# Reordering the head of a fused attention and gated-FFN kernel: new landing assumptions, short holds, a random tie-break, and a last output tile cut 384 and 128 wide

## The chip, the cores and the metric

One core of one Trainium2 chip. The metric is the device time of one execution in microseconds (us). All executions used here are in the fast state. A profile's span, from first to last instruction, is about 1.8 us shorter than the device time of the same execution; spans are compared with spans, times with times.

## The reference

Block-sparse attention with 4 batches, 8 heads, 768 positions and head size 64 feeds a gated FFN. In short:

```python
scores = scale * np.matmul(q, k.transpose(0, 1, 3, 2))
# mask: neighbouring 32-blocks, first and last block, three sampled blocks a row
scores = np.where(mask, scores, -1000000000.0)
attn = np.exp(scores - scores.max(-1, keepdims=True))
attn = attn / (attn.sum(-1, keepdims=True) + 1e-09)
x = np.matmul(attn, v)                      # to 3072 tokens x 512
gate = 1.0 / (1.0 + np.exp(-(x @ w_gate)))
return (gate * (x @ w_val) @ w_out)         # d_ff is 1536
```

## The kernel before

The kernel doesn't write its instructions in the order in which they run. It records operations, each with an engine, an assumed duration and a priority, and its own planner plays them through and gives each engine its order. What the planner assumes of the loads therefore decides where the TensorE's instructions stand; the chip then keeps that order, whatever really lands when. Cut to what matters:

```python
# Plan.run: on each engine, the first ready operation by (priority, place in the program)
for i, o in enumerate(self.ops):
    o.key = (o.prio, i)
...
# if the TensorE has nothing ready, it gets a filler: a matmul on a tile of zeros
if best is None and e == "PE" and now < self.spin_until and ...:
    o = self.spin_op(0.11 if now < 12.0 else 0.06, fresh)
...
# when a load is assumed to have landed
first = now + (2.5 if e == "POOL" else 1.9)
...
o.seen = first + 0.3 + o.slack

# the order of the first loads on one queue (head pairs 0 to 3)
FIRST = [
    ("q", 0), ("k", 1), ("q", 1), ("k", 2), ("q", 2), ("v", 0), ("k", 3), ("q", 3), ("v", 1), ("v", 2), ("v", 3),
]

# the last output tile, two pieces of 256 columns
parts = 2 if last and tt == w // 128 - 1 else 1
wd = DM // parts
for u in range(parts):
    m = slice(u * wd, u * wd + wd)
```

Below, k3 is the k of head pair 3, and so on. A score tile is one third of the keys of one head pair and query group; a value group is the 24 matmuls that follow three exponentials; gate matmuls are those with wg and wv.

The softmax here doesn't subtract the row's maximum and nothing guards it: scores larger than these inputs give would overflow.

Of the kernel before, what the change touches and what calls it, by code (L numbers as in the profile page):

```python
# [22 lines left out]
DM = H * D  # L23
# [4 lines left out]
VW = 66  # L28
SPIN = 22.0
NMASK = 1  # L30
Q0P, M1P, M2P = -39.2, 14, 17
XR, HR = 4, 2
EARLY = [(0, 0), (1, 0), (0, 1), (0, 2), (0, 3)]
FETCH = ((6, 1), (1, 2))
CHAIN, GLAG, OLAG, ROUND = 16, 5, 9, "SoVgggoo"
EDGES = [0, 768, 1536]
LAND = dict(sbi=1.7, mi=1.6, ident=3.2, e0=3.4, e1=3.3, q=3.1, kb=4.4, k=3.5)
FIRST = [
    ("q", 0), ("k", 1), ("q", 1), ("k", 2), ("q", 2), ("v", 0), ("k", 3), ("q", 3), ("v", 1), ("v", 2), ("v", 3),
]  # L40
HALF = [(0, 0), (0, 1), (0, 2), (0, 3)]
TURN_PE = 3
# [19 lines left out]
class Op:  # L62
    def __init__(self, ways, deps, allocs, prio, mode, dma, behind, lands):
        self.ways, self.deps, self.allocs = ways, deps, allocs
        self.prio, self.mode, self.dma, self.behind, self.lands = prio, mode, dma, list(behind), lands
        self.eng = self.start = self.end = self.seen = None
        self.paired = False
        self.slack = 0.0


LAT = {"PE": 0.35, "ACT": 0.2, "DVE": 0.2, "POOL": 0.25, "SP": 0.1}
# [2 lines left out]
class Plan:  # L74
# [35 lines left out]

    def run(self):
        todo = {e: [] for e in LAT}
        for i, o in enumerate(self.ops):
            o.key = (o.prio, i)
            for e in o.ways:
                todo[e].append(o)
        for e in todo:
# [4 lines left out]
        dma_free, mode, order, now = 0.0, None, [], 0.0  # L122
# [48 lines left out]
        while left:  # L171
            wake = []
            for e in LAT:
                if free[e] > now:
                    wake.append(free[e])
                    continue
                best = None
                for o in todo[e]:
                    t = 0.0
                    for d in o.deps:  # L180
                        if d.seen is None:
                            t = None
                            break
                        t = max(t, d.seen if d.eng != e or d.dma else d.end)
                    if t is None or any(d.end is None for d in o.behind):
                        continue
                    if t > now:
                        wake.append(t)
                        continue
                    t, where = places(o.allocs, e)  # L190
                    if t is None:
                        continue
                    if t > now:
                        wake.append(t)
                        continue
                    if o.mode == "row" and mode == "full" and o.paired:
                        s, _ = places([o.allocs[0], o.twin], e)
                        if s is None or s > now:
                            if s is not None:
                                wake.append(s)  # L200
                            if best is None:
                                best = o, where
                            continue
                    best = o, where
                    break
                if best is None and e == "PE" and now < self.spin_until and self.spin.writers[0].seen is not None:
                    if self.spin.writers[0].seen <= now:
                        fresh = self.spun is None or self.rings["ps"][self.spun.slot] is not self.spun
                        o = self.spin_op(0.11 if now < 12.0 else 0.06, fresh)
                        t, where = places(o.allocs, e)  # L210
                        if t is not None and t <= now:
                            best = o, where
                            todo[e].append(o)
                            left += 1
                        elif fresh:
                            self.spun = None
                if best is None:
                    continue
                o, where = best
                take(o, where)  # L220
                o.eng = e
                dur, o.fn = o.ways[e]
                if e == "PE":
                    if o.mode != mode:
                        dur += 0.095
                    mode = o.mode
                o.start, o.end = now, now + dur
                if o.lands is not None:
                    o.seen = o.lands
                    dma_free = max(dma_free, o.lands - 0.3) if e == "POOL" else dma_free  # L230
                elif o.dma:
                    first = now + (2.5 if e == "POOL" else 1.9)
                    if o.dma > 0.15:
                        first = dma_free = max(dma_free, first) + o.dma
                    o.seen = first + 0.3 + o.slack
                else:
                    o.seen = o.end + LAT[e]
                free[e] = o.end
                for w in o.ways:
                    todo[w].remove(o)  # L240
                order.append(o)
                left -= 1
                wake.append(o.end)
            ahead = [w for w in wake if w > now]
            if not ahead:
                if left and not wake:
                    raise RuntimeError("the plan is stuck")
                if left and all(w <= now for w in wake):
                    raise RuntimeError("the plan is stuck")
                continue  # L250
            now = min(ahead)
# [13 lines left out]
def kernel(  # L265
# [11 lines left out]
    nc = tc.nc  # L277
# [21 lines left out]
    P = Plan()  # L299
# [39 lines left out]
    ident16 = one([128, 128], f16, "ident16")  # L339
# [15 lines left out]
    for i, (eng, q, r) in enumerate((("SP", nc.sync, 0), ("ACT", nc.scalar, 64))):  # L355
# [3 lines left out]
            writes=[e24], prio=-93, dma=0.2, lands=LAND[f"e{i}"],  # L359
        ).deps[1:] = []  # L360
    vring = [one([128, 2, NJ, VW], f16, f"v16_{i}") for i in range(8)]
    for i in range(8):
# [3 lines left out]
            writes=[vring[i]], prio=-80 + i,  # L366
# [57 lines left out]
    def load_half(nm, b, p, prio, dur=0.72):  # L424
        cut = (nm, b, p) == ("q", 0, 0)
        js = later if cut else every
        if cut:
            c = one([128, 2, NJ - 2, 64], f16, "q16_late")
        else:
            c = sb(f"{nm}16" if nm != "v" else "vh", [128, 2, NJ, 64], f16)  # L430
        half16[nm, b, p] = stage[nm, b, p] = c
        o = P.op(
            "POOL", dur, lambda: nc.gpsimd.dma_start(c(), src[nm][b][:, 2 * p : 2 * p + 2, js]),  # L433
            writes=[c], prio=prio, dma=0.8 if cut else 1.0,
        )
        o.slack = 0.4 + 0.6 * b
        return o

    def turn_pe(nm, b, p, js, prio, behind=(), c=None, j0=0):
# [47 lines left out]
    P.op("ACT", 0.35, lambda: nc.scalar.copy(q_a(), q_in()), reads=[q_in], writes=[q_a], prio=-88)  # L487
    for i, (nm, p) in enumerate(FIRST):
        last_in = load_half(nm, 0, p, -60 + i)
    late = None  # L490
    for p in range(NP):
        if p == 0:
# [16 lines left out]
    n = 0  # L509
    for a, z in zip(edges, edges[1:]):  # L510
        for nm, t, s in (("g", wg, wgv), ("v", wv, wvv)):

            def go(t=t, s=s, a=a, z=z, nm=nm):
                landed[nm, a] = nc.gpsimd.dma_start(t()[:, :, a:z], s[:, :, a:z])

            o = P.op("POOL", 0.75, go, prio=-37.5 + n * 0.75, behind=[last_in], dma=32 * (0.022 + (z - a) * 0.000124))
            n += 1
            for f in range(a // 128, z // 128):
                w_in[nm, f] = o

    def load_out(s, prio, behind):
        def go():
            ins = nc.gpsimd.dma_start(wo()[:, 4 * s : 4 * s + 4], wov[:, 4 * s : 4 * s + 4])
            if s == 1:
                landed["o"] = ins

        o = P.op(
            "POOL", 0.8, go,
            prio=prio, dma=2.65, behind=behind,
        )  # L530
        for f in range(4 * s, 4 * s + 4):
            w_out[f] = o

# [83 lines left out]
    def attend(n, p, seq):  # L617
        b, c = divmod(n, NCH)
        masked = n < NMASK
        pts = []  # L620
        for tt in range(NCH):
            st, pt = psb([2, 512], homes=PAIR, span=2), sb("pt", [128, 2, 2, CH], f16)

            def scores(tt=tt, st=st):
# [16 lines left out]
                writes=[st], prio=seq, mode="row", behind=scored[-1:],  # L641
            )
            if (n, p, tt) == (0, 0, 0):
# [8 lines left out]
                reads=[st], writes=[pt], prio=seq,  # L652
# [14 lines left out]
        def values():  # L667
# [9 lines left out]
                        )  # L677

        valued[n, p] = P.op("PE", 0.79, values, reads=[*pts, v16[b, p]], writes=[o], prio=seq + (3.05 if n == 0 and p < 3 else 0.1), mode="full")
        P.op("DVE", 0.2, lambda: nc.vector.reciprocal(rz(), o()[:, :, 64:65]), reads=[o], writes=[rz], prio=seq - 5)  # L680
        P.op(
            "DVE", 0.36,
            lambda: nc.vector.tensor_tensor(  # L683
# [3 lines left out]
                op=ALU.mult,  # L687
            ),
            reads=[o, rz], writes=[x16], prio=seq - 5,
        )  # L690
        g, i = group_of[n]
        dst = xT[g, p]
        if n >= TURN_PE:
# [11 lines left out]
        def turn():  # L705
# [1 line left out]
            for jq in range(2):  # L707
                nc.tensor.transpose(tT()[:, jq, :], x16()[:, jq, :], ident16())  # L708

        P.op("PE", 0.12, turn, reads=[x16, ident16], writes=[tT, dst], prio=seq - 5, mode="full")  # L710
        P.op(
            "DVE", 0.28,
            lambda: nc.vector.tensor_copy(  # L713
                dst()[:, i * CH : (i + 1) * CH], tT().rearrange("p j q -> p (j q)")
            ),
            reads=[tT], writes=[dst], prio=seq - 5,
        )


    hts, gates, outs = {}, [], []  # L720
# [1 line left out]
    def ffn(g, seq):  # L722
# [42 lines left out]
        for tt in range(w // 128):  # L765
            n, jq = GROUPS[g][tt // 2], tt % 2
            b, c = divmod(n, NCH)
            y = sb("y", [128, DM], f32)
            parts = 2 if last and tt == w // 128 - 1 else 1
            wd = DM // parts  # L770
            for u in range(parts):
                m = slice(u * wd, u * wd + wd)
                py = psb([DM])
                for f0 in range(0, NF, 2):

# [112 lines left out]
```

## Time and profile before

| what | value |
|---|---|
| time, median of 3 | 292.07 us (291.51 to 292.13) |
| span of the profile | 290.4 us |
| TensorE busy | 284.0 us, 98% |
| first score matmul, first gate matmul | 6.47 us, 28.74 us |
| first output matmul of the third group | 90.53 us |
| start of the last matmul to the end | 3.38 us |

The starts are read off the TensorE's timeline. The prediction shows the lines of the page, the waits and the chain.

### The profile page before, as it was taken

The page shows a single profiled execution, that of the slowest core. Times are in us where ns is not written, and L with a number is a line of the kernel's source. Part 1 is how long each engine was busy: PE and PEld are TensorE (multiplying, and loading weights), DVE is VectorE, ACT ScalarE, POOL GpSimd, SP SyncE. Part 2 cuts the span into 40 slices and gives each one's busy share as a digit, 9 for nine tenths or more (in the row PEclk, how much of TensorE's full clock was granted, in tenths as well). Part 3 has the DMA queues.
Part 4 walks back from the last instruction along what each step waited for, and adds up shares of the span by engine and source line. Part 5 has one row for each costly group of instructions (what it writes and reads, how often), then busy time and mean ns, then how long its engine had stood idle before and what let it go on. Part 6 is the DMA issues. An engine that isn't in the chain of part 4 may idle for free.

```text
span 290.4 us, 8113 instructions
## 1 busy us (share of the span) xinstructions
PE 284.0 (98%) x3410; PEld 211.8 (73%) x3410; DVE 192.5 (66%) x448; ACT 211.1 (73%) x330; POOL 14.9 (5%) x24
## 2 busy tenths in 40 slices
PE   7899999999999999999999999999999999999995
PEld 6576876787687677777777767767777777777763
DVE  3778979778775767657857867756765765763230
ACT  2958689988957778678779779678768777772331
POOL 8740000000000000000000000000000000000000
PEclk9999999999999999999999999999999999999999
DMA  7999999996686484015286686011011010111003
GB/s 112 176 208 210 208 250 225 274 257 208 142 198 208 61 232 84 19 47 205 50 236 144 167 238 102 18 47 45 18 50 42 14 56 23 36 56 45 9 30 109
DMA packets 50788, 35.30 MB, mean 122 GB/s; under 512 B 31376, under 2 KB 47808, under 8 KB 50752
## 3 DMA queue, kind: packets, MB, share of 16 engines
q1 hardware_dynamic: 43304, 27.71, 37.1%
q0 software_dynamic: 7232, 7.01, 15.0%
q8 instruction: 26, 0.43, 0.6%
q14 instruction: 10, 0.08, 0.1%
q10 hardware_dynamic: 216, 0.07, 0.1%
HBM read 28.42 MB, written 6.29 MB: 120 GB/s over the span
## 4 chain that ended last, share of the span: by engine, by line
PE 93%; DMA 3%; POOL 2%; DVE 1%; issue 0%; ACT 0%; POOLq 0%
PE psum L734 44%; PE psum L778 23%; PE psum L672 13%; PE psum L631 12%; DMA k<-in_k_dram 3%; PE psum L708 1%; PE psum L451 1%; POOL k L433 0%; POOL q L433 0%; PE psum L593 0%; POOL k_a L480 0%; POOL q_late L433 0%; POOL k_b L484 0%; POOL vh L433 0%; DVE mask L601 0%
## 5 line engine op out<-in xcount | busy, mean ns | idle before, releaser
L649 ACT ACTIVATE pt<-psum 128x1024 f16<-128x1024 f32 x144 | 138.2, 1031 | 20.6 <-PE psum L631 20.5
L657 DVE TENSOR_TENSOR pt<-pt,mask 128x1024 f16<-128x1024 f16 x132 | 89.0, 688 | 50.1 <-ACT pt L649 50.0
L734 PE MATMUL psum<-x,wv 128*128 128x256 f16 x576 | 86.4, 273 | 0.0
L734 PE MATMUL psum<-x,wg 128*128 128x256 f16 x576 | 86.3, 272 | 0.0
L753 ACT ACTIVATE tg<-psum 128x256 f32<-128x256 f32 x144 | 56.4, 393 | 39.3 <-PE psum L734 39.2
L760 DVE SCALAR_TENSOR_TENSOR h<-tg,psum 128x256 f16<-128x256 f32 x144 | 58.2, 417 | 26.0 <-ACT tg L753 25.5
L778 PE MATMUL psum<-wo,h 128*128 128x512 f16 (+1 forms) x300 | 75.1, 372 | 0.0
L734 PEld LDWEIGHTS <-wv 128*128 128x128 f16 x576 | 56.0, 98 | 7.0 <-issue 0.6
L734 PEld LDWEIGHTS <-wg 128*128 128x128 f16 x576 | 53.5, 98 | 7.3 <-issue 0.6
L672 PEld LDWEIGHTS <-pt 128*128 128x128 f16 x1152 | 42.4, 98 | 9.4 <-issue 0.8
L631 PE MATMUL psum<-qT,kT 64*128 64x256 f16 x576 | 44.3, 271 | 0.3 <-DVE x L713 0.3
L672 PE MATMUL psum<-v,pt 128*128 128x65 f16 x1152 | 44.5, 193 | 0.0
L778 PEld LDWEIGHTS <-h 128*128 128x128 f16 x300 | 26.2, 98 | 23.1 <-issue 7.4
L631 PEld LDWEIGHTS <-kT 64*128 64x128 f16 x576 | 24.5, 94 | 19.5 <-issue 15.9
L795 ACT ACTIVATE y<-psum 128x512 f32<-128x512 f32 (+1 forms) x24 | 13.9, 579 | 13.0 <-PE psum L778 13.0
L683 DVE TENSOR_TENSOR x<-psum,rz 128x256 f16<-128x256 f32 x48 | 20.3, 424 | 1.5
L680 DVE RECIPROCAL rz<-psum 128x4 f32<-128x4 f32 x48 | 8.6, 179 | 3.5 <-PE psum L672 3.4
L374 PE MATMUL psum<-zero 128*64 128x128 f16 x40 | 5.4, 300 | 1.0 <-DVE zero L344 1.0
L601 DVE TENSOR_SCALAR mask<-psum 128x512 f16<-128x512 f32 x9 | 6.2, 686 | 0.3 <-PE psum L593 0.2
L631 PE MATMUL psum<-bias,e 64*128 64x256 f16 x48 | 6.1, 275 | 0.0
L421 ACT CAST q<-qs 128x768 f16<-128x768 f32 x7 | 5.9, 849 | 0.0
L374 PEld LDWEIGHTS <-zero 128*64 128x64 f16 x40 | 4.3, 163 | 1.7 <-DVE zero L344 1.0
(54 smaller groups left out, 72.1 us busy)
## 6 DMA issues: line engine op xcount, KB each, us to landing
out_dram<-y SPq DMA_DIRECT2D x23, 256.0 KB, 2.4
ks<-in_k_dram SPq DMA_DIRECT2D x12, 384.0 KB, 3.6
qs<-in_q_dram SPq DMA_DIRECT2D x12, 384.0 KB, 4.3
vs<-in_v_dram SPq DMA_DIRECT2D x12, 384.0 KB, 5.7
wg<-in_moe_w_gate_dram POOLq DMA_DIRECT2D x2, 768.0 KB, 14.3
wv<-in_moe_w_val_dram POOLq DMA_DIRECT2D x2, 768.0 KB, 16.4
wo<-in_moe_w_out_dram POOLq DMA_DIRECT2D x3, 512.0 KB, 22.3
vh<-in_v_dram POOLq DMA_DIRECT2D x4, 192.0 KB, 7.8
```

The source lines that it names most:

```text
L374: "PE", dur, lambda: nc.tensor.matmul(t()[0:64], zero()[:, 0:64], zero(), start=True, stop=True),
L631: nc.tensor.matmul(st()[:, hd, jj * CH : (jj + 1) * CH], l[r, 2 * tt + jj, :], m[r, 2 * c : 2 * c + 2, :], start=not (own and masked), sto ...
L649: lambda st=st, pt=pt: nc.scalar.activation(pt().rearrange("p h j q -> p h (j q)"), st(), AF.Exp, scale=SCALE),
L657: nc.vector.tensor_tensor(t, t, mask()[:, c, tt].unsqueeze(1).to_broadcast([128, 2, 512]), op=ALU.mult)
L672: nc.tensor.matmul(o()[:, 2 * jq + hd, 0:65], pts[j // 2]()[:, hd, j % 2, jq * 128 : jq * 128 + 128], v_[:, hd, j, 0:65], start=(j == 0), ...
L680: P.op("DVE", 0.2, lambda: nc.vector.reciprocal(rz(), o()[:, :, 64:65]), reads=[o], writes=[rz], prio=seq - 5)
L683: lambda: nc.vector.tensor_tensor(x16().rearrange("p j (h d) -> p (j h) d", d=64), o()[:, :, 0:64], rz().to_broadcast([128, 4, 64]), op=AL ...
L734: nc.tensor.matmul(t()[:, z : z + w], wt()[:, i, f * 128 : (f + 1) * 128], xT[g, i]()[:, 0:w], start=(i == 0), stop=(i == NP - 1),)
L753: lambda tg=tg, a=pair[0]: nc.scalar.activation(tg()[:, 0:w], a[0]()[:, a[1] : a[1] + w], AF.Tanh, scale=0.5),
L760: lambda tg=tg, a=pair[1], h_=h_: nc.vector.scalar_tensor_tensor(h_()[:, 0:w], tg()[:, 0:w], 1.0, a[0]()[:, a[1] : a[1] + w], op0=ALU.add, ...
L778: nc.tensor.matmul(py()[:, m], hts[g, f]()[:, tt * 128 : (tt + 1) * 128], wo()[:, f, m], start=(f == 0), stop=(f == NF - 1),)
L795: lambda py=py, y=y, m=m: nc.scalar.activation(y()[:, m], py()[:, m], AF.Copy, scale=0.5),
```

## The change

The intent is to plan with landing times closer to what was measured, so that the TensorE meets no load that has not landed: more slack for the loads of the first batch and of the weights (a little less, 0.7 instead of 1.0, for the second batch's), v1 fetched before k3 and q3, and engines that wait up to 0.4 us for the operations that follow a value group of the first query group, rather than let others overtake them. A fixed random draw breaks ties between priorities. The last output tile is cut so that less is left after the last matmul. The core of the diff, with cuts marked by "...":

```diff
+SEED, MIX = 17, 0.4
-XR, HR = 4, 2
+XR, HR, HOLD, HN = 4, 2, 0.4, 1
...
-    ("q", 0), ... ("q", 2), ("v", 0), ("k", 3), ("q", 3), ("v", 1), ("v", 2), ("v", 3),
+    ("q", 0), ... ("q", 2), ("v", 0), ("v", 1), ("k", 3), ("q", 3), ("v", 2), ("v", 3),
...
+        mix = np.random.default_rng(SEED).normal(0.0, MIX, len(self.ops))
         for i, o in enumerate(self.ops):
-            o.key = (o.prio, i)
+            o.key = (o.prio + (mix[i] if -45 < o.prio < 60 else 0.0), i)
...
+                        if t <= now + o.hold:
+                            break
...
-        o.slack = 0.4 + 0.6 * b
+        o.slack = 0.7
...
+        last_in.slack = 0.7 if i < 6 else 1.7
...
+            o.slack = 2.0          # the loads of wg, wv and wo
...
+        hold = HOLD if n < HN else 0.0   # on the four operations after a value group
...
-            parts = 2 if last and tt == w // 128 - 1 else 1
-            wd = DM // parts
-            for u in range(parts):
-                m = slice(u * wd, u * wd + wd)
+            cuts = [0, 384, DM] if last and tt == w // 128 - 1 else [0, DM]
+            for a, z in zip(cuts, cuts[1:]):
+                m, parts = slice(a, z), DM / (z - a)
```

More of the change, by code (lines that the diff above doesn't have):

```diff
@@ L38 @@
 FIRST = [
-    ("q", 0), ("k", 1), ("q", 1), ("k", 2), ("q", 2), ("v", 0), ("k", 3), ("q", 3), ("v", 1), ("v", 2), ("v", 3),
+    ("q", 0), ("k", 1), ("q", 1), ("k", 2), ("q", 2), ("v", 0), ("v", 1), ("k", 3), ("q", 3), ("v", 2), ("v", 3),
 ]
@@ L67, in __init__ @@
         self.paired = False
-        self.slack = 0.0
+        self.slack = self.hold = 0.0
 LAT = {"PE": 0.35, "ACT": 0.2, "DVE": 0.2, "POOL": 0.25, "SP": 0.1}
@@ L530, in load_out @@
         )
+        o.slack = 2.0
         for f in range(4 * s, 4 * s + 4):
@@ L679, in attend @@
         valued[n, p] = P.op("PE", 0.79, values, reads=[*pts, v16[b, p]], writes=[o], prio=seq + (3.05 if n == 0 and p < 3 else 0.1), mode="full")
-        P.op("DVE", 0.2, lambda: nc.vector.reciprocal(rz(), o()[:, :, 64:65]), reads=[o], writes=[rz], prio=seq - 5)
+        hold = HOLD if n < HN else 0.0
+        P.op(
+            "DVE", 0.2, lambda: nc.vector.reciprocal(rz(), o()[:, :, 64:65]), reads=[o], writes=[rz], prio=seq - 5
+        ).hold = hold
         P.op(
@@ L689, in attend @@
             reads=[o, rz], writes=[x16], prio=seq - 5,
-        )
+        ).hold = hold
         g, i = group_of[n]
@@ L708, in turn @@
                 nc.tensor.transpose(tT()[:, jq, :], x16()[:, jq, :], ident16())
-        P.op("PE", 0.12, turn, reads=[x16, ident16], writes=[tT, dst], prio=seq - 5, mode="full")
+        P.op("PE", 0.12, turn, reads=[x16, ident16], writes=[tT, dst], prio=seq - 5, mode="full").hold = hold
         P.op(
@@ L716, in attend @@
             reads=[tT], writes=[dst], prio=seq - 5,
-        )
+        ).hold = hold
     hts, gates, outs = {}, [], []
```

## The prediction

> **What bounds the kernel now.** I began with the page's busy shares and slices, to see whether one engine is full and where it is not.
>
> ```profile
> span 290.4 us, 8113 instructions
> ...
> PE 284.0 (98%) x3410; PEld 211.8 (73%) x3410; DVE 192.5 (66%) x448; ACT 211.1 (73%) x330; POOL 14.9 (5%) x24
> ...
> PE   7899999999999999999999999999999999999995
> ...
> PEclk9999999999999999999999999999999999999999
> ```
>
> The TensorE is busy in nearly all of every slice from the fourth to the last but one, at full clock. Only the first three slices (22 us) and the last show any slack. Busy is not the same as useful, so I next asked for the waits of the TensorE, in the whole run and from 40 us on. The second answer is empty; the first is this:
>
> ```profile
> PE psum L451 <- DMA k<-in_k_dram: 1.1, 1, 1.1
> PE psum L374 <- DVE zero L344: 1.0, 1, 1.0
> PE psum L569 <- DMA e<-bb_e: 0.6, 1, 0.6
> PE psum L593 <- ACT pt L649: 0.3, 1, 0.3
> PE psum L631 <- DVE x L713: 0.3, 1, 0.3
> ```
>
> The waits for the zero tile and for e are the start, which the change leaves as it is. What is left is 1.1 us for the k of the fourth head pair (k3) and twice 0.3 us. The chain of work in order of time shows where they stand and what the end is made of:
>
> ```profile
> 7.01 7.69 DMA k<-in_k_dram
> 14.70 0.04 issue
> 14.75 0.53 PE psum L451 x12
> 15.27 0.87 PE psum L672 x24
> ...
> 27.27 0.60 DVE mask L601
> 27.88 0.21 DVE x L713
> 28.08 0.04 issue
> 28.13 0.68 PE psum L631 x8
> 28.81 0.98 PE psum L734 x8
> ...
> 281.20 6.09 PE psum L778 x40
> ```
>
> The first gate matmuls (L734) start at 28.7 us, and from there the chain is TensorE alone down to the last output tile; after it come one 0.38 us eviction (287.31 to 287.69) and the last store, issued at 287.72 and landed at 289.42. So the kernel is a fixed amount of TensorE work, a head of 28.7 us with some holes, and a tail of 3.1 us. The change can win only the holes and part of the tail.
>
> A hole need not show as idle: matmuls on a tile of zeros (L374) fill time in which the kernel's own planner expects the TensorE to wait. After the first 33 of them, at the start, the timeline has seven, which is the other soft spot.
>
> **What the Trainium skill says.** "Perfetto Trace Analysis", section "Identifying the Most-Contended Engine", warns that matmul busy time is a poor measure of distance to the roofline, and advises weight-load busy time beside it. It is 73% here, so I did not take the 98% as proof, but the empty list of waits. "TensorE: Matmul & The Clock Gate", section "Back-to-back issue gap", gives N/2.4 + 2.5 ns between warm matmuls of width N. The trace agrees: groups of four 256-wide matmuls start 0.437 us apart, 0.109 each. The same section names 81 ns for a sustained stream of 128-wide matmuls with weight loads; the value matmuls (L672, 65 wide, a load each) take 0.76 us for 24, 32 ns, so the trace shows no such floor for narrower ones. "DMA: Bandwidth & Descriptors", section "Anatomy of one DMA — SWDGE (gpsimd) path", has a fixed cost of about 2.0 us. The last store goes through another path and took 1.70 us from the start of its issue, so here the trace decides.
>
> **The change, part by part.** All arithmetic is kept. The planner's assumptions change (landing slack, holds, a random term in the priorities), and with them the order on each engine. I read the order of both builds.
>
> (a) v1 is fetched before k3 and q3. In the trace before, the ninth to eleventh loads of that queue landed at 14.70 (k3), 15.20 (q3) and 16.14 us (v1). If places keep their times, v1 lands at 14.7, k3 at 15.2, q3 at 16.1. Alone this makes the k3 wait longer. But the TensorE order now puts the first value group (0.87 us by the chain), two masked score tiles (0.98 for 16 matmuls) and the third mask tile (0.22) ahead of k3's transposes. Before reached that point at 13.62 us; 13.62 + 0.87 + 0.98 + 0.22 and about 0.3 of filler make 16.0, my estimate, 0.8 after k3 lands. The 1.13 us wait goes: **-1.13**.
>
> (b) The two 0.3 us waits near 27.5 us: in the new order one mask tile and one score tile move behind the first gate matmuls, and on the VectorE one 0.6 us mask copy no longer lies between the normalisation of head pair 3 and its copy (L713), which releases the first gates. But DVE is busy 4.83 and 4.93 of 5 us in the windows 25 to 30 and 30 to 35, so some of the wait may return. I chose half of the 0.56: **-0.3**.
>
> (c) Filler matmuls go from 40 to 46, all six more in the head. Three of them in a row took from 9.80 to 10.08, 0.09 each. Where the wait they fill is real they cost nothing; I chose two thirds of 0.54 as cost: **+0.35**.
>
> (d) Changes of TensorE mode (row-packed scores, column-packed transposes, full) go from 127 to 131; up to the first gate matmul they are equal (35 and 35). One costs about 0.096: four 512-wide matmuls took from 88.81 to 89.77, 0.96 instead of 4 x 0.216 = 0.864. Four more: **+0.38**. After the first output matmuls of the third group (90.5 us in before) the orders are the same.
>
> (e) Last tile 384 and 128 wide instead of twice 256. TensorE: 12 x 0.218 is the same sum, as 12 x 0.163 + 12 x 0.056 by the skill's formula is 2.63 against 2.62. The last eviction: 597 ns for 512 columns and 383 for 256 give 0.84 ns a column, hence 276 ns for 128, -0.11. The last store is 64 KB instead of 128: 256 KB took 2.05 us (282.72 to 284.77), 128 KB 1.70, so perhaps -0.17. But the 384-wide piece now ends about 0.67 us before the last, and its store is in flight beside the last one. I chose **-0.15** of the 0.28.
>
> (f) New small waits that I can't see from an order: **+0.1**.
>
> Sum: -1.13 - 0.3 + 0.35 + 0.38 - 0.15 + 0.1 = -0.75 us. 292.07 - 0.75 = **291.3 us**.
>
> **The rivals.** First, ScalarE or VectorE is the head's real bound, and the won time turns into waits for exponentials. For it: the first nine exponentials run without a gap from 7.17 to 15.53 us, and DVE is full from 25 to 35. Against it: ACT then waits 1.43, 0.24, 1.30 and 0.96 us for scores, so it has room of nearly 4 us before 26.5. This would leave about 292.0.
>
> Second, k3 or q3 lands later than its place suggests (loads are spaced about 1.0 us, k3's gap was 2.09), or filler and mode changes cost full price. For it: the margin of (a) is only 0.8. Then the wait is partly kept, with +0.9 of (c) and (d): 292.2.
>
> Third, all goes well: both waits vanish whole, fillers lie only in real waits, the tail gives its 0.28. Then -1.13 - 0.56 + 0.38 - 0.28 = -1.6, so 290.5. That a fixed random draw was kept speaks for an order chosen because it measured well.
>
> Fourth, for the tail: at 81 ns a matmul the 128-wide piece would take 0.97 us instead of 0.67, and the tail would lose 0.3 rather than win 0.15: 291.7.
>
> **Range and chances.** The rivals span 290.5 to 292.2; the three runs of before span 0.6 us by themselves. I take 290.4 to 292.2. Two per cent is 5.8 us. Holes that the change can touch sum to about 2 us, so faster by that is next to impossible (0.01); slower by it would need several waits of the k3 kind in the later head (0.01); within 2%: 0.98.
>
> **What would show it right or wrong.** (a) No wait for k3 or q3 among the TensorE's waits, and k3 landing near 15.2. (b) First gate matmul near 27.3 us with one score and one mask tile fewer before it, 0.44 us of work; a start after 28.2 means no gain in the head. (c) and (d) The start of the first output matmul of the third group, 90.5 before, near 89.9. (e) 128-wide matmuls 56 ns apart, last eviction 0.28 us, and the time from the last matmul to the end 0.15 shorter. The prediction is wrong if the ACT's gaps between 15 and 27 us remain and the TensorE shows new waits for exponentials, or if new waits appear after 30 us, where before had none.

## The result, and the profile after

The changed kernel took 291.97 us (median of 4, 291.80 to 292.09), the kernel before 292.10 us beside it (median of 4). A ratio is the mean time of one kernel's executions over the mean of the other's of the same rounds, so it isn't quite the ratio of these medians: 0.9998, with a 95% interval of 0.9981 to 1.0015. No difference is to be seen. A repeat of the same kernel, `after_again` below, gave 1.0033.

The page of the changed kernel, span and busy times:

```profile
span 290.1 us, 8127 instructions
...
PE 284.3 (98%) x3416; PEld 211.1 (73%) x3416; DVE 193.1 (67%) x451; ACT 209.1 (72%) x327; POOL 14.8 (5%) x24
```

The TensorE is as full as before. Its waits in the whole run (engine and line, what it waited for, us in total, times, longest):

```profile
PE psum L378 <- DVE zero L348: 1.0, 1, 1.0
PE psum L576 <- DMA e<-bb_e: 0.5, 1, 0.5
PE psum L455 <- DMA k_b<-in_k_dram: 0.5, 1, 0.5
PE psum L718 <- DVE x L693: 0.3, 1, 0.3
PE psum L638 <- ACT pt L656: 0.2, 1, 0.2
PE psum L679 <- ACT pt L656: 0.2, 1, 0.2
```

The 1.1 us wait for k3 is gone, as intended. In place of the two waits of 0.3 us near 27.5 us stand three of 0.27, 0.18 and 0.19. From 40 us on there are none. The chain of work in order of time (start, us, what):

```profile
5.60 6.00 DMA q<-in_q_dram
11.60 0.04 issue
11.64 0.30 PE psum L455 x4
...
12.70 0.17 PE psum L378
...
15.98 0.46 PE psum L455 x12
...
20.19 0.28 PE psum L378 x3
...
22.69 1.94 ACT pt L656 x2
24.63 0.04 issue
24.68 0.92 PE psum L679 x24
...
26.41 0.98 ACT pt L656
27.39 0.04 issue
27.43 0.39 PE psum L638 x4
27.82 1.42 PE psum L744 x12
```

This view holds the main reading. Before, the chain came out of the load of k3. Now it comes out of the load of q2, which landed at 11.60, and runs through the TensorE, two exponentials (22.69), the TensorE again and a third exponential (26.41) to the first gate. So exponentials are on the chain of the new order; in the old one there was none between the load and the first gate (VectorE was on it, from 26.03 to 28.08). k3's transposes (15.98) stand in its middle without a wait. The fillers (L378) are on it too.

The tail. First the last ACT evictions of the kernel before, then those of the changed kernel, from the timelines:

```profile
286.00 0.38 ACT L795 ACTIVATE y<-psum 128x256 f32<-128x256 f32 x1 [0.71 <-PE psum L778]
287.31 0.38 ACT L795 ACTIVATE y<-psum 128x256 f32<-128x256 f32 x1 [0.93 <-PE psum L778]
```

```profile
286.52 0.49 ACT L804 ACTIVATE y<-psum 128x384 f32<-128x384 f32 x1 [1.35 <-PE psum L787]
287.19 0.28 ACT L804 ACTIVATE y<-psum 128x128 f32<-128x128 f32 x1 [0.18 <-PE psum L787]
```

The last eviction shrank from 0.38 to 0.28 us, and the last store, issued at 287.49, landed at 289.11.

Where the 0.31 us between the two spans (290.39 and 290.08) come from, from the timelines; "fillers" is the time from each filler to the next matmul less waits, and both are between first score and first gate:

| stretch | before | after | difference |
|---|---|---|---|
| to the first score | 6.47 | 6.27 | -0.20 |
| first score to first gate | 22.27 | 21.49 | -0.78 |
| ... of it waits | 1.69 | 0.86 | -0.83 |
| ... of it fillers (7 and 13) | 1.06 | 1.74 | +0.68 |
| first gate to first output matmul of group 3 | 61.79 | 62.65 | +0.86 |
| from there to the end | 199.86 | 199.67 | -0.19 |

In the changed kernel one mask tile and one score tile, four matmul steps of 0.109 us, or 0.44, stand behind the first gate rather than ahead of it. So the stretch from the first score to the first gate really won 0.34, and the one behind it really lost 0.42.

### The profile page after: what moved, and what is told of

Same layout as the page of the kernel before. It is cut to its first block, busy times and chain, and to the rows that moved or that the text cites. A ratio compares the mean times of both kernels' runs of the same rounds, so it can differ in the third digit from the quotient of the medians.

```text
span 290.1 us, 8127 instructions
## 1 busy us (share of the span) xinstructions
PE 284.3 (98%) x3416; PEld 211.1 (73%) x3416; DVE 193.1 (67%) x451; ACT 209.1 (72%) x327; POOL 14.8 (5%) x24
## 4 chain that ended last, share of the span: by engine, by line
PE 94%; DMA 2%; POOL 2%; ACT 1%; issue 1%; ACTq 0%; POOLq 0%
PE psum L744 44%; PE psum L787 23%; PE psum L638 13%; PE psum L679 13%; DMA q<-in_q_dram 2%; ACT pt L656 1%; PE psum L455 1%; PE psum L718 1%; PE psum L600 0%; POOL k L437 0%; POOL k_a L484 0%; PE psum L378 0%; POOL q L437 0%; POOL q_late L437 0%; POOL k_b L488 0%
## 5 line engine op out<-in xcount | busy, mean ns | idle before, releaser
L787 PE MATMUL psum<-wo,h 128*128 128x512 f16 (+2 forms) x300 | 75.5, 372 | 0.0
L804 ACT ACTIVATE y<-psum 128x512 f32<-128x512 f32 (+2 forms) x24 | 13.9, 580 | 12.6 <-PE psum L787 12.6
L378 PE MATMUL psum<-zero 128*64 128x128 f16 x46 | 6.0, 276 | 1.0 <-DVE zero L348 1.0
L378 PEld LDWEIGHTS <-zero 128*64 128x64 f16 x46 | 4.4, 146 | 2.1 <-issue 1.1
```

The lines of the kernel that those rows point to most:

```text
L378: "PE", dur, lambda: nc.tensor.matmul(t()[0:64], zero()[:, 0:64], zero(), start=True, stop=True),
L787: nc.tensor.matmul(py()[:, m], hts[g, f]()[:, tt * 128 : (tt + 1) * 128], wo()[:, f, m], start=(f == 0), stop=(f == NF - 1),)
L804: lambda py=py, y=y, m=m: nc.scalar.activation(y()[:, m], py()[:, m], AF.Copy, scale=0.5),
```

## The experiments

Twelve kernels ran, in three series of four. The kernel before ran 11 times beside each: medians 292.32, 292.29 and 292.36 us. The series ran on three different chips (7, 12 and 0), and the changed kernel as it is ran only in the first; so times are compared within a series, and what is said across series is weaker.

**First series: repeat, tail alone, scores earlier, no late fillers.** `after_again` has no edit.

> The changed kernel once more, beside the kernel before on the same chip, to see how far two profiles and two sets of runs of it differ. All theories: ratio to before 0.998 to 1.001; first gate matmul near 27.8 us, first output matmul of the third group near 90.4 us (before 90.53), no wait for k3. If these points move by more than 0.3 us, single profiles can't carry the account.

It took 293.31 us (median of 5, 292.43 to 293.52), ratio 1.0033 (1.0017 to 1.0048). The profiled execution was one of the two short ones, with a span of 290.7; the others were 290.5, 291.5, 291.6 and 291.6. The kernel before had 289.9 to 290.8 beside it. The first gate came at 28.33 and the third group's first output matmul at 90.98, both 0.57 later than in the first profile. So the expectation missed: one profile can't carry the account, and something moves the whole run by half a microsecond and more. For the traced executions the second series shows what it is.

`b_tail384` is the kernel before with the new tail:

```diff
-            parts = 2 if last and tt == w // 128 - 1 else 1
+            cuts = [0, 384, DM] if last and tt == w // 128 - 1 else [0, DM]
```

> The kernel before with the last output tile cut 384 and 128 wide, nothing else. Prediction's term: the head stays as before, last matmul to end about 0.2 us shorter (3.38 us before, 3.15 in the changed kernel), ratio 0.9993. Rival (two stores in flight collide, or 128-wide matmuls at 81 ns): no gain or a loss of 0.1 to 0.3 us.

291.85 us, ratio 0.9989 (0.9971 to 1.0006). The time alone doesn't decide, but the trace does: from the start of the last matmul to the end it took 3.13 us instead of 3.38, and the 128-wide matmuls started 56 ns apart, so the rival of 81 ns falls. The last start lies 0.05 later in its stretch, since the last matmul is shorter; net 0.19 to 0.20. Two stores in flight did not collide enough to cost that.

`a_feed` moves two masked score tiles earlier on the TensorE, in the changed kernel, after the plan is made:

```diff
+        s, st = P.tags["S", 0, 2, 2]        # third score tile of head pair 2
+        st.slot = 4                         # banks that are free by then
+        put(s, valued[0, 1])                # right after the second value group
+        put(P.tags["E", 0, 2, 2], P.tags["E", 0, 2, 1])
+        # first score tile of head pair 3: ahead of the late transposes of q3
```

> The changed kernel with two masked score tiles moved ahead on the TensorE alone: the third tile of head pair 2 to just after the second value group, the first of head pair 3 to just before the late transposes of q3. Nothing added or taken. Theory F (the won time was lost because scores come late, the exponentials starve for 2.14 and 1.08 us, and value groups, copies and gates wait for them later): the two ACT gaps shrink to under 0.6 us together less than 1.2, the TensorE waits for exponentials (0.2 and 0.2) go, the first output matmul of the third group comes at 90.0 instead of 90.41, and the time falls by 0.3 to 0.5 us against the changed kernel. Theory M (it was lost to six more fillers and four more mode changes, and the TensorE is simply full): ACT gaps shrink, but that matmul stays at 90.3 to 90.4 and the time within 0.1 us.

292.29 us, ratio 1.0006 (0.9989 to 1.0023). The two ACT gaps fell from 2.14 and 1.08 to 0.48 and 0.62, but a third of 1.52 came behind them, and the third group began at 90.83, not 90.0. By these numbers alone theory F would fall. But q2 landed at 11.98 here, later than the 11.60 of the first profile, and the first gate came at 27.72, 15.74 after it; in both profiles of the unedited kernel it came 16.16 after. So the earlier scores did win 0.42 us in the head, as F says. From there to the gate matmuls at 53.21 the two kernels keep step, and there the gain is lost again, 0.47 us, in a wait that the unedited kernel doesn't have:

```profile
53.21 0.60 PE L748 MATMUL psum<-x,wg 128*128 128x256 f16 x4 [0.31 <-ACT pt L660]
```

The chain leads from that exponential back to a later load of q, which landed at 51.33; in the two profiles of the unedited kernel it landed at 49.33 and 49.47. So what hid the gain at the third group looks to be a late load of this one execution. Against the 293.31 of the unedited kernel the time is lower, as F expected, but that series scatters by 1.1 us and has three long executions. So this run bears F out for the head and leaves the time open; it doesn't refute F.

`a_nofill` drops the fillers after the plan's 8 us mark:

```diff
         for o in order:
+            if o.prio == 1e6 and o.start > 8.0:
+                continue
             o.fn()
```

> The changed kernel without the filler matmuls on zeros that the plan puts after its 8 us mark (10 of 46); all other instructions in the same order. Fillers took 1.74 us between the first score and the first gate in the changed kernel, 1.06 before. Theory M (fillers cost their full length): the time falls by 0.6 to 0.9 us, the idle time of the TensorE in the head stays at 0.9. Theory F (they mostly lie in time that would be waited anyway, behind exponentials and loads): idle grows by at least half of what the fillers took, the time falls by 0.1 to 0.4 us. Third possibility: the TensorE clock falls without them and the time rises.

291.56 us, ratio 0.9982 (0.9967 to 0.9997): faster than the kernel before, and by more than 1 us than the changed kernel of this series. In the profile, idle time between first score and first gate rose from 0.86 to 2.02 while fillers fell from 1.74 to 0.55. One wait of 1.0 us was for q2, which landed at 12.35: the fillers ahead of q2's transposes had only covered it. Those behind it cost their length, as the account below shows. (With the ten fillers 8 changes of TensorE mode went too, 131 to 123; the time of a filler given here, to the start of the next matmul, includes them.) So M is right for one part of them and F's half (idle grows) for the other.

**Second series: is the wait for k3 a property of the order?** `before_again` has no edit.

> The kernel before once more. Theory L (the 1.1 us wait for k3 that the prediction booked as a gain was partly an accident of that one execution, as the loads land up to 0.7 us apart from run to run and the long gap in the queue sits now before k3, now before q3): the wait for k3 is under 0.6 us or absent in this profile, or the first gate comes within 0.4 us of 28.1 as in the run with the new tail only. Rival (the wait belongs to the order): k3 lands near 14.7 again and the wait is 1.0 to 1.2 us. Ratio 0.999 to 1.001.

292.26 us, ratio 0.9994 (0.9969 to 1.0018). In its profiled execution, k3 landed at 13.98, and the TensorE, whose last filler ended at 13.97, waited 0.05 us for it, not 1.13. (The waits list has 0.3 us for a k, but that is k1, which landed at 9.08.) That span was 289.6, the other five 290.5 to 290.8. The chain of this execution:

```profile
7.03 6.95 DMA k<-in_k_dram
13.98 0.04 issue
14.02 0.53 PE psum L451 x12
```

k3's load is the start of the chain again, 0.72 us earlier. Theory L is right about this execution; the spans of the others, close to the 290.4 of the first profile, suggest that the late k3 is the common case. They have no traces; in the three other traces of this order (`b_tail384`, `b_nofill_tail`, `before_cold`) k3 landed at 14.05, 14.19 and 13.52, so none repeats the 14.70.

Of the changed kernel's second profile, the chain begins with q2 as in the first:

```profile
5.61 6.56 DMA q<-in_q_dram
12.17 0.04 issue
12.21 0.30 PE psum L455 x4
```

This gives the account that the first theories had missed. In both orders there is one load from whose landing to the end the chain is fixed, k3 in the old order and q2 in the new one:

| profile | load on the chain, landed | first gate | group 3 begins | from landing to group 3 |
|---|---|---|---|---|
| before | k3, 14.70 | 28.74 | 90.53 | 75.83 |
| before, again | k3, 13.98 | 28.02 | 89.80 | 75.82 |
| after | q2, 11.60 | 27.75 | 90.41 | 78.81 |
| after, again | q2, 12.17 | 28.33 | 90.98 | 78.81 |
| after, more early fillers (below) | q2, 13.69 | 29.85 | 92.50 | 78.81 |

The last column is constant to 0.01 us within an order. (In `b_tail384`, also in the old order, it is 75.88: there q3, landed at 15.43, held its transposes up by 0.06.) The new order needs 78.81 - 75.83 = 2.98 us more after its load, and that load comes two places earlier in the queue than k3 did. Within one execution of the old order, q2 and k3 landed 3.03 us apart (11.67 and 14.70) in the first profile, and 1.92 (12.06 and 13.98) in the second. If q2 lands in the new order when it did in these, the change wins 0.05 us at this point in the first case and loses 1.06 in the second (an estimate from the table); the tail adds a gain of 0.19 to either.

`b_nofill_tail` is the kernel before with the new tail and without fillers after the 8 us mark (the edits shown above).

> The kernel before with the new last tile and without the fillers after the plan's 8 us mark (34 instead of 40). If the two gains are separate and add: tail 0.25 us, fillers up to 0.5 us, 291.4 to 291.9 where before is 292.3, ratio 0.997 to 0.9985. If fillers cover real waits here: the tail's 0.25 alone, 0.9990.

291.74 us, ratio 0.9980 (0.9955 to 1.0005), within the range for gains that add; the interval just includes 1. With k3 landed at 14.19, group 3 began at 89.63, 75.44 later: 0.39 less than 75.83. Of this, 0.34 are the two fillers behind k3's transposes, 0.17 each on the chain of the kernel before. In `a_nofill` the same difference is 90.22 - 12.35 = 77.87, 0.94 less than 78.81; there the six fillers behind q2 took 0.79 on the chain. This kernel in the old order ends up with the same ratio as `a_nofill` in the new one (0.9980 and 0.9982, both with the new tail): without late fillers the reordering shows no gain of its own.

`b_first` changes the order of loads alone:

```diff
-    ... ("v", 0), ("k", 3), ("q", 3), ("v", 1), ("v", 2), ("v", 3),
+    ... ("v", 0), ("v", 1), ("k", 3), ("q", 3), ("v", 2), ("v", 3),
```

> The kernel before with v1 fetched ahead of k3 and q3 and nothing else changed in the text (the planner then orders the head anew: 38 fillers, 128 mode changes). Theory of the prediction: the queue order is what removes the wait for k3, so this alone brings 0.5 to 1.0 us (ratio 0.9965 to 0.998). Theory L: it brings 0 to 0.3 us, ratio 0.999 to 1.0005.

292.90 us, ratio 1.0020 (0.9996 to 1.0044): no gain, against the prediction's theory, and above the range of L too. The planner makes another order of it. In the profiled execution, the slowest of the six, the TensorE waited 1.25 us, for q1's transposes; k3's met no wait:

```profile
11.01 0.30 PE L451 MATMUL psum<-ident,q 128*64 128x128 f16 x4 [1.25 <-ACT pt L649]
...
16.00 0.53 PE L451 MATMUL psum<-ident,k 128*64 128x128 f16 x12
```

The view names an exponential, which ended at 10.98. But q1 itself landed at 10.97, 2.89 us after k1, and the weight loads of these transposes are listed as waiting 1.5 us for it; so late a load explains the wait as well. So the wait for k3 went here too, and another one before it took its place. This run doesn't isolate the fetch order, as the planner moved much else (its group 3 began at 91.89).

`a_mix0` sets the random draw to nothing:

```diff
-SEED, MIX = 17, 0.4
+SEED, MIX = 17, 0.0
```

> The changed kernel without the random draw (ties fall in the order of the program; 44 fillers, 133 mode changes; the third score tile of head pair 2 follows k3's transposes at once). If the draw was what made the change good: 0.3 to 0.6 us slower than the changed kernel, near 292.6 or more. If late scores were what cost it the gain: 0.3 us faster. By mode changes alone (two more): 0.2 us slower.

293.27 us, ratio 1.0023 (0.9999 to 1.0048), like the 293.31 of the changed kernel in the first series. The draw is not shown to be worth anything, nor to have cost anything. Its profile has something else: the TensorE's clock came to full speed only after 10 us. In the other nine profiles so far it came between 4.4 and 6.6. The span was 291.6.

**Third series: what a late clock and a late load do to each order.** `before_cold` and `after_cold` drop the 34 fillers before the plan's 6 us mark, so that the clock comes late in both:

```diff
         for o in order:
+            if o.prio == 1e6 and o.start < 6.0:
+                continue
             o.fn()
```

> The kernel before without the 34 fillers before the plan's 6 us mark, so that the TensorE does nothing until 4.5 us and its clock comes to full speed late (it came at 4.4 to 6.6 us in nine of the ten profiles so far, and after 10 us in one, whose span was 291.6). Theory A (absorbed): in the old order the TensorE must wait for k3 at 13.4 us in most executions, so a TensorE that is about 1 us slower up to 10 us only eats that wait: first gate within 0.4 us of 28.7, time within 0.5 us of before. Rival (both orders lose alike): 0.8 to 1.3 us slower, as much as the changed kernel without these fillers.

292.28 us, ratio 1.0007 (0.9995 to 1.0019). All six spans lie between 290.3 and 290.9. Matmuls are slow up to 10.8 us, and k3's transposes still start at 14.62, where in the first profile, with a fast clock, they started at 14.75. Three lines of the TensorE's timeline show it, a score step at the slow clock, one at the fast clock, and k3's transposes:

```profile
6.24 0.42 PE L633 MATMUL psum<-qT,kT 64*128 64x256 f16 x2
...
12.77 0.27 PE L633 MATMUL psum<-qT,kT 64*128 64x256 f16 x2
...
14.62 0.57 PE L453 MATMUL psum<-ident,k 128*64 128x128 f16 x12
```

There is no wait for k3 in this execution. But k3 landed early, at 13.52, and the TensorE came 1.1 us after it, so this trace doesn't show the slow clock hidden behind a late k3. What bears theory A out for the old order are the times: no loss beside the kernel before.

> The changed kernel without the same 34 fillers. Theory A: nothing in the new order waits for the queue after 12 us, so a late clock goes straight to the end: first gate near 29.0 as in the run without the draw, span 291.3 to 291.9, time 1.0 to 1.6 us above the changed kernel's fast executions, and at least 0.6 us more loss than the old order shows. Rival: the same loss as the old order, within 0.3 us.

292.98 us, ratio 1.0028 (1.0016 to 1.0040), spans 290.8 to 291.6; first gate at 28.54 in the profile, not 29.0; three of the five spans lie below the expected 291.3 to 291.9. The difference to the old order without early fillers is 0.70 us. The part of theory A that tells the two apart held, at its lower edge; against the changed kernel's executions (291.97 in the first series) the loss is 1.0, but that is a comparison across series. The third group began 79.49 after q2 landed (11.70) rather than 78.81: here q2 was not on the chain, which leads from k_b's load (5.78) through slow matmuls to 9.68 and then through VectorE's copies and masks to 13.39. By this count the late clock cost 0.68 us. The time, 1.0028, does not show it by itself: the same kernel with early fillers had 0.9998 once and 1.0033 in the repeat.

`after_warm` adds ten fillers in the first two gaps of the changed kernel, to bring the clock early:

```diff
         for o in order:
+            if o.prio == 1e6:
+                fill += 1
+                for _ in range({26: 6, 31: 4}.get(fill, 0)):
+                    o.fn()
             o.fn()
```

> The changed kernel with ten more fillers in the two first idle gaps of the TensorE (six before the mask expansion, four before k_b's transposes), to make the clock come early in every execution. If the executions of 291.5 us span among the changed kernel's are late clocks: all spans below 291.0, median time 0.3 to 1.0 below the 293.3 of its second series, spread under 0.8 us. If the clock comes by a phase that activity can't move, or loads are the cause: spans of 291.5 again.

292.55 us, ratio 1.0022 (1.0004 to 1.0040). Five spans are 290.6 to 291.0, none near 291.5; the profiled one is 292.2, with the clock early, at 4.3 us. Its waits say why:

```profile
PE psum L460 <- DMA q<-in_q_dram: 1.2, 1, 1.2
...
PE psum L460 <- DMA k<-in_k_dram: 0.9, 1, 0.9
```

The loads were late in this execution (k1 at 9.59, q2 at 13.69), and the whole run was late by the same amount; it is the last row of the table above. So loads alone can do what the late clock can. That the 291.5 us executions of `after_again` were late clocks fits, but they have no traces, and it stays open.

`a_nofill_warm` has both edits, more fillers early and none late.

> Both edits that looked good on the changed kernel: ten more fillers in the first gaps and none after the plan's 8 us mark. Without late fillers alone 291.56 us (before 292.32 beside it). If the two add: 291.2 to 291.5, ratio 0.996 to 0.9975, a version that beats both kernels. If the late fillers' saving is all there is: 0.998.

291.68 us (291.29 to 291.87), ratio 0.9982 (0.9970 to 0.9994), spans 289.5 to 290.1. The saving is that of the late fillers (in the profile, from q2's landing to group 3 it took 78.05, 0.76 less than 78.81); the early ones add nothing to it that the times show. It beats the kernel before beside it by 0.18%, and the interval excludes 1. This and `a_nofill` are the only versions of which that can be said; `a_nofill` also beat the changed kernel of its own series.

| run | median us | ratio to before (95%) |
|---|---|---|
| after, first series / again | 291.97 / 293.31 | 0.9998 (0.9981-1.0015) / 1.0033 (1.0017-1.0048) |
| b_tail384 | 291.85 | 0.9989 (0.9971-1.0006) |
| a_feed | 292.29 | 1.0006 (0.9989-1.0023) |
| a_nofill | 291.56 | 0.9982 (0.9967-0.9997) |
| before_again | 292.26 | 0.9994 (0.9969-1.0018) |
| b_nofill_tail | 291.74 | 0.9980 (0.9955-1.0005) |
| b_first | 292.90 | 1.0020 (0.9996-1.0044) |
| a_mix0 | 293.27 | 1.0023 (0.9999-1.0048) |
| before_cold / after_cold | 292.28 / 292.98 | 1.0007 (0.9995-1.0019) / 1.0028 (1.0016-1.0040) |
| after_warm | 292.55 | 1.0022 (1.0004-1.0040) |
| a_nofill_warm | 291.68 | 0.9982 (0.9970-0.9994) |

## Why the prediction was right or wrong

The time, 291.97, lies in the range 290.4 to 292.2, and "within 2%" was right. That says little, as the range held the unchanged 292.07 too. The gain of 0.75 did not come: the medians beside each other differ by 0.1, and the repeat had a loss of 0.3%. The prediction's own signs of being wrong came: hardly a gain at the third group (90.41, not 89.9), gaps of 2.14 and 1.08 us left on ACT between 15 and 27 us, and new waits for exponentials. By its steps:

**What bounds the kernel.** Right: TensorE without a wait from the first gate on, in every profile of the two kernels.

**(a) The wait for k3, -1.13.** The wait went, and k3 landed at 15.42, near the 15.2 predicted. The step that failed is "The 1.13 us wait goes: -1.13". It took the wait of one execution for a property of the order: in another execution of the same kernel it was 0.05, as k3 landed 0.72 earlier and the TensorE, held up by k1 and q1, came 0.35 later. And it took the end of one wait for the same gain at the end. The load on the chain became q2, from which the new order has 2.98 us more to do than the old one has from k3; what is won is the distance of two loads less 2.98. The rivals named a wait for exponentials, a later k3 and fillers, but no earlier load.

**(b) The two later waits, -0.3.** Wrong in sign. 0.56 us became 0.64 in three other places, two of them for exponentials, as the first rival had it. That rival holds in part: three exponentials are on the new chain, and `a_feed` brought the first gate 0.42 us nearer to q2's landing by feeding them earlier.

**(c) Fillers, +0.35.** Mis-sized: they took 0.68 more between the first profiles. Behind the load on the chain they cost their full length, as `a_nofill` and `b_nofill_tail` show (0.94 and 0.39 us, a difference of 0.55); those ahead of it cost nothing. The step took 0.09 for a filler from three in a row; alone between matmuls of another mode, one takes 0.17.

**(d) Mode changes, +0.38.** Right: 0.42 once the moved work is taken off, the same in both profiles of the changed kernel.

**(e) The tail, -0.15.** Right: -0.19, 56 ns between the 128-wide matmuls, 0.28 us for the last eviction.

**(f) Small new waits, +0.1.** They are in (b).

With (b) as +0.08, (c) as 0.68, (d) as 0.42 and (e) as -0.19, even a full -1.13 for (a) would leave -0.14, close to the 0.13 between the two medians. The margins for fillers and later waits were each chosen on the hopeful side. (A small slip of reading: the page's digits show slack in the first two slices and the last, not in three.)

**Why the repeat was slower.** This is not shown, as its three long executions have no traces. Two causes are at hand: a later q2, which the traces show to move the whole run one for one, and a late clock. A slow clock up to 10 us costs the old order nothing that the times show (`before_cold`, ratio 1.0007); the new order had no late wait to hide it, and the trace of `after_cold` has it 0.68 us late. "TensorE: Matmul & The Clock Gate", section "What's actually happening", says that the clock follows a free-running activity window, so that its coming varies from run to run, by about half a microsecond either way. The profiles agree that it varies, but more widely: with early fillers in the program it came between 4.3 and 6.6 us, and once after 10. If so, a removed wait is also a removed buffer against such luck. How often each case comes in untraced executions is open.

## What to carry to other kernels

Before booking a wait as a gain, ask what the chain will start from once it is gone, and work out the distance from there to the end; two landings subtract, and the wait itself is not in the formula. Look at a second execution's trace before a wait on a load is taken as part of the order. Where a scheduler fills expected idle time with dummy work, test without the part of it that stands behind the load on the chain: here that was worth 0.2%, in the old order as in the new, and more than all of the reordering. And look up in the timeline which instruction a wait in a list belongs to: k1 and k3, or two loads of q, share one line there.

## What the Trainium skill lacked or had wrong

- "DMA: Bandwidth & Descriptors" gives a fixed cost and a rate for a load, and nothing on how far one load's landing moves from one execution to the next. Here k1 landed between 8.1 and 9.6 us and q2 between 11.6 and 13.7, with the same issue times; most loads followed each other by about 1.0 us, with a longer gap of 1.4 to 2.9 us at changing places (before k3: 2.09 us in one execution of the kernel before, 0.98 in another).
- The same page's fixed cost of about 2.0 us is given for the GpSimd path; for the SyncE path it gives no such fixed cost. A store of 64 KB from the SyncE landed 1.26 us after its issue ended and 1.62 after it began.
- "TensorE: Matmul & The Clock Gate", section "Back-to-back issue gap", has 81 ns for a sustained stream of 128-wide matmuls with weight loads. The last piece's twelve started 56 ns apart, each with its own load, which is what the page gives for the isolated gap.
- "TensorEngine Tiling (Array Packing)", section "Key Properties", says that changing the tiling mode drains the TensorE, but not what it costs. Here it was about 0.1 us a change (0.42 us for four).
- No page ties the cost of a late clock to the order behind it: beside the kernel before, the order with a later wait showed none (1.0007, interval includes 1), and in the trace of the one without, the third group came 0.68 us later than q2's landing alone would have it.
